# Linear attention and a GELU feed-forward block on one core: where the loads of batch 4 are issued

## The chip, the core and the metric

The kernel runs on one core of a Trainium2 chip. A core has five engines with queues of their own: PE (TensorE, matrix products into PSUM), DVE (VectorE), ACT (ScalarE), POOL (GpSimd) and SP (SyncE, which here issues nearly all DMAs). [...] The metric is the device time of one execution in microseconds, the median of several runs.

## The reference

For 8 batches, 8 heads, 576 positions and a head size of 64:

```python
q_s = softmax(q, axis=-1)          # over the 64 elements of a head
k_s = softmax(k, axis=2)           # over the 576 positions
kv  = einsum('bhsd,bhse->bhde', k_s, v)      # 64 x 64 per head
x   = einsum('bhsd,bhde->bhse', q_s, kv)     # then (4608 tokens, 512)
h   = x @ w_in                               # 512 -> 2048
g   = 0.5 * h * (1 + erf(h / sqrt(2)))       # exact GELU
out = g @ w_out                              # 2048 -> 512
```

All inputs and the output are float32. The kernel works in bfloat16 inside and accumulates in float32.

## The kernel before

**Chunks.** The 4608 tokens are cut into nine chunks of 512. Chunks 0 to 7 hold the first 512 positions of each batch, chunk 8 the last 64 positions of all eight. For each chunk there are two long phases on PE. `h_phase(c)` (matmuls at L295) computes the 16 column blocks of `x @ w_in`, four matmuls each, and ACT applies GELU to each block (L300) into `g`. `y_phase(c)` (matmuls at L305) computes four output groups `j` of 16 matmuls each, `g @ w_out`. The end of each group is `y_out(c, ps, j)`: DVE copies the group from PSUM to SBUF (`y_sb`, L312), and SP sends it to DRAM (L315). The PSUM pool `psum_y` of these groups has two buffers, so group `j` needs the buffer of group `j - 2`. The SBUF pool of `y_sb` has four.

**The attention of the next batches** is put between these matmuls. For a batch `b`:

- `load(b)` issues three DMAs on SP: q (L90), k and v (both L98). Each of the three names has two SBUF buffers, so batch `b` takes the buffers of batch `b - 2`.
- `exp_q(b)` and `exp_k(b)` (L133, L138) run on ACT, between the GELUs of two chunks, since ACT must load another function table for them.
- `cast_v_all(b)` (L145) converts v to bfloat16 in four DVE instructions.
- `norm_q(b)` sums (L196) and inverts (L197) on DVE and multiplies on POOL or DVE (L198).
- `xbar_step(b)` (L231) transposes the normalised q by a DMA that SP issues; its result is `qT`.
- `kv_step(b)` computes `kv` on PE (L166) and normalises it on DVE; `x_all(b)` multiplies `qT` with it on PE (L251), and DVE and ACT copy the result out as `xT`, which the next `h_phase` reads.

**The order is written by hand.** The program runs under a manual schedule: each engine executes its own instructions in the order in which the Python code emits them, and SP's DMAs too. `ins` names, for a block of the `h_phase`, or for a pair (group, matmul) of the `y_phase`, the functions that are emitted right behind it. From chunk 2 on the loop at L555 sets these places: loads two batches ahead at the start of `h_phase(c)`, `cast_v_all` behind matmul 8 of the first output group, `norm_q` behind the first matmul of the second group, `xbar_step` behind the first of the fourth, and `x_all` and `kv_step` within the third. Chunk 1's output phase (L538) has a plan of its own, because it finishes batch 2 and starts batch 3 there. Chunk 2 begins with `front3` (L549), which normalises and transposes batch 3 and issues `load(4)`.

SP's order around the change is, before: output (1,0), transpose of batch 2, outputs (1,1), (1,2) and (1,3), transpose of batch 3, `load(4)`, output (2,0). Here (1,2) stands for output group 2 of chunk 1.

Of the kernel before, what the change touches and what calls it, by code (L numbers as in the profile page):

```python
# [16 lines left out]
def kernel(  # L17
# [65 lines left out]
    def load_main(b, name, t, parts=1):  # L83
        f = f32in.tile([128, 2048], FP32, tag=name + "f")
        f = f.rearrange("p (h f) -> p h f", h=H)
        st[b][name + "f"] = f
        src = t[b, :, 0:M, :].rearrange("h (p j) d -> p h (j d)", j=J)
        n = H // parts
        for i in range(parts):
            nc.sync.dma_start(out=f[:, i * n:(i + 1) * n, :], in_=src[:, i * n:(i + 1) * n, :])  # L90

    def load_pair(b, name, t, parts=1):
        f = f32in.tile([128, HP, NS * D], FP32, tag=name + "f")
        st[b][name + "f"] = f
        src = t[b].rearrange("h (p n) d -> (h p) (n d)", n=NS).rearrange("(x q) f -> q x f", q=128)
        n = HP // parts
        for i in range(parts):
            nc.sync.dma_start(out=f[:, i * n:(i + 1) * n, :], in_=src[:, i * n:(i + 1) * n, :])  # L98

    def load(b):  # L100
        load_main(b, "q", q)
        load_pair(b, "k", k)
        load_pair(b, "v", v)
# [40 lines left out]
    def cast_v(b, hp, eng=nc.vector):  # L144
        eng.tensor_copy(  # L145
            out=v_aug[b % 2][:, hp, :, 0:D],
            in_=st[b]["vf"][:, hp, :].rearrange("p (n d) -> p n d", n=NS),
        )

    def cast_v_all(b):  # L150
        for hp in range(HP):
            cast_v(b, hp)
# [30 lines left out]
    def kv_step(b):  # L183
        kv_mm(b, 0)
        kv_mm(b, 1)
        kv_norm(b, 0, 2)

    def norm_q(b, i=0, n=1, eng=None):

        eng = eng or nc.gpsimd  # L190
        eq = st[b]["eq"]
        w = H // n
        hs = slice(i * w, (i + 1) * w)
        qsum = small.tile([128, J, w], FP32, tag="qsum")
        recq = small.tile([128, J, w], FP32, tag="recq")
        nc.vector.reduce_sum(out=qsum, in_=eq[:, :, hs, :], axis=AX.X)  # L196
        nc.vector.reciprocal(recq, qsum)  # L197
        eng.tensor_tensor(  # L198
            out=eq[:, :, hs, :], in0=eq[:, :, hs, :],
            in1=recq.unsqueeze(3).to_broadcast([128, J, w, D]), op=ALU.mult,  # L200
        )
# [27 lines left out]
    def xbar_step(b):  # L229
        st[b]["qT"] = attn_sb.tile([128, J, HP, 128], BF16, tag="qT", name="qT")  # L230
        nc.sync.dma_start_transpose(  # L231
            out=st[b]["qT"].rearrange("p j x m -> p (j x) m"),
            in_=st[b]["eq"].rearrange("p j h d -> p (j h d)"),
        )
# [27 lines left out]
    def x_all(b):  # L262

        for hp in range(HP):
            pool, tag = (psum_h, "h") if hp < 3 else (psum_a, "a")
            x_tile(b, hp, pool, tag)
        x_mm(b, 0)
        x_mm(b, 1)
        for hp, eng in ((0, "s"), (2, "v"), (1, "s"), (3, "v")):
            x_evac(b, hp, eng)  # L270
# [233 lines left out]
    def y_end(j):  # L504
# [35 lines left out]
        (1, 1): [lambda: norm_q(2, 1, 2, nc.vector)],  # L540
        (1, 12): [lambda: kv_step(2)],
        (1, 15): [lambda: xbar_step(2)],
        (2, 2): [lambda: cast_v_all(3)],
        (3, 5): [lambda: x_all(2), lambda: kv_step(3)],
    })

# [2 lines left out]
    def front3():  # L549
        norm_q(3, 0, 2)  # L550
        norm_q(3, 1, 2, nc.vector)
        xbar_step(3)
        load(4)

    for c in range(2, B + 1):  # L555
        nb = c + 2
# [54 lines left out]
```

The softmax here doesn't subtract the row's maximum and nothing guards it: scores larger than these inputs give would overflow.

## Time and profile before

| | |
|---|---|
| median of 3 runs | 283.63 us (283.61 to 283.81) |
| profiled execution, its own time | 283.85 us |
| its span, from the first to the last instruction | 282.0 us |
| PE busy | 272.0 us (96%) |
| ACT busy | 156.8 us (56%) |
| DVE busy | 102.1 us (36%) |
| granted PE clock | 1.0 throughout |
| one load of a batch: q, k, v | 1024, 1152 and 1152 KB |
| median time from issue to landing: q, k, v | 7.2, 9.8 and 11.5 us |
| one output group | 256 KB, 2.3 us to landing |
| one transposing DMA | 3.8 us to landing |

All times inside the profile are microseconds from the start of the span. A row of instruction groups reads: line, engine, operation, output <- inputs, shape, count; then the busy time and the mean of one in ns; then the idle time of the engine just before, and who ended it. A row of the waits reads: who waited for whom, in total, how often, the longest. A row of a timeline reads: start, duration, engine, line, operation, count, and in brackets the idle time of the engine before it. PE's matmuls are pipelined and their ends are modelled, so a stretch that is listed as busy can end some tenths of a microsecond late.

### The profile page before, as it was taken

To read this page: it belongs to the slowest core of one execution; us is meant where nothing else is said; L and a number is where in the kernel's file an instruction comes from. 1 tells how busy PE (TensorE), PEld (TensorE's weight loads), DVE (VectorE), ACT (ScalarE), POOL (GpSimd) and SP (SyncE) were. 2 spreads that over 40 slices of the span, in tenths; PEclk is the share of its full clock that TensorE was granted. 3 is DMA by queue.
4 is the path that set the end of the run, shared out by engine and by line. 5 is a ranking of instruction groups with operands and counts; after the bars stand their busy time and mean duration, and the time that the engine had idled before them with its cause. 6 is when DMAs were issued, how large, how long until landed. Compare 5 with 4: busy or idle time off the path is not lost.

```text
span 282.0 us, 4555 instructions
## 1 busy us (share of the span) xinstructions
PE 272.0 (96%) x1922; PEld 125.8 (45%) x1922; DVE 102.1 (36%) x150; ACT 156.8 (56%) x242; POOL 32.9 (12%) x25
## 2 busy tenths in 40 slices
PE   7789999999999899999999999999999999999993
PEld 3334454444444344444444444444444444444442
DVE  3766486309750560084007500651016100220021
ACT  5856754689377815693469446853683363136300
POOL 0620050002020050005000500050005000000000
PEclk9999999999999999999999999999999999999999
DMA  7999999952439339911991189117501500210033
GB/s 233 387 404 431 397 401 406 402 219 68 124 103 360 132 114 248 349 38 42 241 377 52 40 200 361 76 73 185 115 0 74 149 2 0 77 74 0 0 77 76
DMA packets 44852, 50.10 MB, mean 178 GB/s; under 512 B 20384, under 2 KB 29856, under 8 KB 44576
## 3 DMA queue, kind: packets, MB, share of 16 engines
q1 hardware_dynamic: 44544, 49.68, 51.8%
q8 instruction: 15, 0.25, 0.3%
q10 hardware_dynamic: 288, 0.13, 0.2%
q14 instruction: 5, 0.04, 0.0%
HBM read 36.70 MB, written 9.44 MB: 164 GB/s over the span
## 4 chain that ended last, share of the span: by engine, by line
PE 81%; DMA 10%; DVE 3%; ACT 2%; SPq 1%; issue 1%; ACTq 0%
PE ps L305 39%; PE ps L295 38%; DMA f<-in_v_dram 6%; DMA w<-in_moe_w_in_dram 3%; PE kv L166 2%; DMA f<-in_q_dram 1%; PE ps L251 1%; PE ps L327 1%; DVE v_aug L145 1%; DVE qsum L196 1%; ACT ek L138 1%; ACT e L133 1%; DVE e L198 1%; SPq L231 0%; DVE y_sb L312 0%
## 5 line engine op out<-in xcount | busy, mean ns | idle before, releaser
L295 PE MATMUL ps<-xT,wi_bf 128*128 128x512 bf16 x576 | 126.1, 379 | 1.0 <-DVE wi_bf L379 1.0
L305 PE MATMUL ps<-wo_bf,g 128*128 128x512 bf16 x560 | 124.4, 379 | 1.1 <-DVE y_sb L312 1.1
L300 ACT ACTIVATE g<-ps 128x512 bf16<-128x512 f32 x144 | 85.6, 597 | 68.4 <-PE ps L295 68.4
L295 PEld LDWEIGHTS <-wi_bf 128*128 128x128 bf16 x576 | 56.2, 98 | 69.3 <-DVE wi_bf L379 1.5
L305 PEld LDWEIGHTS <-g 128*128 128x128 bf16 x560 | 53.9, 98 | 65.5 <-issue 1.8
L312 DVE COPY y_sb<-ps 128x512 f32<-128x512 f32 x35 | 23.9, 684 | 74.9 <-PE ps L305 74.6
L198 POOL TENSOR_TENSOR e<-e,recq 128x2048 bf16<-128x2048 bf16 (+1 forms) x9 | 25.7, 2856 | 179.1 <-DVE recq L197 147.1
L145 DVE CAST v_aug<-f 128x576 bf16<-128x576 f32 x26 | 17.9, 745 | 57.1 <-DMA f<-in_v_dram 57.1
L277 ACT CAST xT<-ps 128x512 bf16<-128x512 f32 x19 | 10.2, 589 | 31.3 <-PE ps L251 21.7
L196 DVE TENSOR_REDUCE qsum<-e 128x16 f32<-128x1024 bf16 (+1 forms) x13 | 21.0, 1614 | 14.8 <-ACT e L133 14.8
L133 ACT ACTIVATE e<-f 128x512 bf16<-128x512 f32 (+1 forms) x42 | 20.5, 556 | 2.0 <-DMA f<-in_q_dram 1.7
L138 ACT ACTIVATE ek<-f 128x2304 bf16<-128x2304 f32 (+1 forms) x10 | 17.2, 1730 | 1.7 <-DMA f<-in_k_dram 1.7
L275 DVE CAST xT<-ps 128x512 bf16<-128x512 f32 x15 | 9.7, 687 | 15.4 <-PE ps L251 12.6
L79 ACT ACT_TABLE_LOAD x9 | 11.5, 1283 | 2.8 <-issue 2.6
L405 PE MATMUL ps<-zeros 128*128 128x512 f32 (+1 forms) x14 | 8.3, 734 | 1.5 <-DVE zeros L436 1.5
L133 ACT ACT_TABLE_LOAD x7 | 9.0, 1283 | 0.1
L379 DVE CAST wi_bf<-w 128x512 bf16<-128x512 f32 (+1 forms) x8 | 7.1, 909 | 2.8 <-DMA w<-in_moe_w_in_dram 2.8
L166 PEld LDWEIGHTS <-ek 64*64 64x64 bf16 x576 | 6.5, 105 | 2.9 <-issue 1.1
L166 PE MATMUL kv<-v_aug,ek 64*64 64x65 bf16 x576 | 7.1, 193 | 0.1
L398 DVE CAST wo_bf<-w 128x2048 bf16<-128x2048 f32 (+1 forms) x5 | 5.1, 1011 | 4.1 <-DMA w<-in_moe_w_out_dram 4.1
L198 DVE TENSOR_TENSOR e<-e,recq 128x1024 bf16<-128x1024 bf16 x4 | 6.4, 1610 | 0.1
L251 PE MATMUL ps<-qT,kvc 64*64 64x512 bf16 x60 | 5.0, 390 | 1.0 <-DVE kvc L177 1.0
(33 smaller groups left out, 41.6 us busy)
## 6 DMA issues: line engine op xcount, KB each, us to landing
out_dram<-y_sb SPq DMA_DIRECT2D x32, 256.0 KB, 2.3
f<-in_k_dram SPq DMA_DIRECT2D x6, 1152.0 KB, 9.8
f<-in_v_dram SPq DMA_DIRECT2D x6, 1152.0 KB, 11.5
f<-in_q_dram SPq DMA_DIRECT2D x6, 1024.0 KB, 7.2
w<-in_moe_w_in_dram SPq DMA_DIRECT2D x6, 512.0 KB, 8.9
f<-in_k_dram SPq DMA_DIRECT2D x4, 576.0 KB, 10.0
f<-in_v_dram SPq DMA_DIRECT2D x8, 288.0 KB, 7.7
f<-in_q_dram SPq DMA_DIRECT2D x4, 512.0 KB, 8.6
```

Source lines behind the costliest of these rows:

```text
L79: nc.scalar.activation(out=scr[:, 1:2], in_=scr[:, 0:1], func=func)
L133: nc.scalar.activation(out=dst[:, i], in_=src[:, u], func=AF.Exp)
L138: nc.scalar.activation(out=ek[b % 2][:, i:i + n], in_=st[b]["kf"][:, i:i + n].rearrange("p x (n d) -> p x n d", n=NS), func=AF.Exp,)
L145: eng.tensor_copy(out=v_aug[b % 2][:, hp, :, 0:D], in_=st[b]["vf"][:, hp, :].rearrange("p (n d) -> p n d", n=NS),)
L166: nc.tensor.matmul(ps[c, i, half, 0:D + 1], ek[b % 2][pr, hp, n, :], v_aug[b % 2][pr, hp, n, 0:D + 1], start=(n == 0), stop=(n == NS - 1),)
L196: nc.vector.reduce_sum(out=qsum, in_=eq[:, :, hs, :], axis=AX.X)
L198: eng.tensor_tensor(out=eq[:, :, hs, :], in0=eq[:, :, hs, :], in1=recq.unsqueeze(3).to_broadcast([128, J, w, D]), op=ALU.mult,)
L277: nc.scalar.copy(out=st[b]["xT"][:, hp, :], in_=ps)
L295: nc.tensor.matmul(ps, wi_bf[:, dm, t * 128:(t + 1) * 128], xT[:, dm, :], start=(dm == 0), stop=(dm == NDM - 1),)
L300: nc.scalar.activation(out=g[:, t, :], in_=ps, func=AF.Gelu)
L305: nc.tensor.matmul(ps, st[c]["g"][:, t, j * 128:(j + 1) * 128], wo_bf[:, t, :], start=(t == 0), stop=(t == NDF - 1),)
L312: nc.vector.tensor_copy(out=y_sb, in_=ps)
```

## The change

`load(4)` is issued in the third output group of chunk 1, behind its third matmul and the four casts of batch 3's v. Before, it was issued in the first block of chunk 2's `h_phase`, behind the transpose of batch 3. The three DMAs are the same, and no instruction is added or removed. In SP's order they now stand behind output (1,1) and ahead of outputs (1,2) and (1,3) and of the transpose of batch 3.

```diff
@@ y_phase(1, ...)
         (1, 12): [lambda: kv_step(2)],
         (1, 15): [lambda: xbar_step(2)],
-        (2, 2): [lambda: cast_v_all(3)],
+        (2, 2): [lambda: cast_v_all(3), lambda: load(4)],
         (3, 5): [lambda: x_all(2), lambda: kv_step(3)],
     })
@@ front3, called behind the first block of h_phase(2)
         norm_q(3, 0, 2)
         norm_q(3, 1, 2, nc.vector)
         xbar_step(3)
-        load(4)
```

## The prediction

> **What bounds the kernel now.** I read the page first, then the waits of TensorE, then the chain that ended last in order of time, then the timelines of PE and SP around the change. The page's first part, and its row for the second product (the `y` matmuls):
>
> ```profile
> PE 272.0 (96%) x1922; PEld 125.8 (45%) x1922; DVE 102.1 (36%) x150; ACT 156.8 (56%) x242; POOL 32.9 (12%) x25
> ...
> L305 PE MATMUL ps<-wo_bf,g 128*128 128x512 bf16 x560 | 124.4, 379 | 1.1 <-DVE y_sb L312 1.1
> ```
>
> PE is busy for 96% of the span at full clock. No other engine passes 56%. So the time moves only if an idle stretch of PE goes away or a new one appears. All of PE's listed waits:
>
> ```profile
> PE ps L405 <- DVE zeros L436: 1.5, 1, 1.5
> PE ps L305 <- DVE y_sb L312: 1.1, 1, 1.1
> PE ps L295 <- DVE wi_bf L379: 1.0, 1, 1.0
> PE ps L251 <- DVE kvc L177: 1.0, 2, 0.6
> PE ps L212 <- POOL e L198: 0.9, 1, 0.9
> ```
>
> The second is a single stall. The chain in order of time shows what is behind it (start us, us, what):
>
> ```profile
> 81.74 1.33 SPq L231
> ...
> 83.12 0.64 SPq L90
> ...
> 83.81 0.70 SPq L98
> ...
> 84.55 10.19 DMA f<-in_v_dram
> ...
> 94.76 2.73 DVE v_aug L145 x4
> 97.49 0.61 DVE y_sb L312
> ...
> 98.14 2.97 PE ps L305 x13
> ```
>
> These are the three DMAs of `load(4)` (L90 is q, L98 is k and then v), issued behind the transposing DMA of batch 3 (L231). `v` lands at 94.74. DVE casts it at once (`cast_v_all(4)`, four casts, 2.73 us), and only then copies out the first `y` group of chunk 2 (L312). PE's third group needs that group's PSUM buffer, since `psum_y` has two, and waits for it. The PE timeline of chunks 2, 3 and 4 gives the size of the loss:
>
> ```profile
> 89.95 7.07 PE L305 MATMUL ps<-wo_bf,g 128*128 128x512 bf16 x32
> 98.14 2.97 PE L305 MATMUL ps<-wo_bf,g 128*128 128x512 bf16 x13 [1.13 <-DVE y_sb L312]
> ...
> 106.35 13.98 PE L295 MATMUL ps<-xT,wi_bf 128*128 128x512 bf16 x64
> 120.16 9.88 PE L305 MATMUL ps<-wo_bf,g 128*128 128x512 bf16 x45
> ...
> 135.28 13.98 PE L295 MATMUL ps<-xT,wi_bf 128*128 128x512 bf16 x64
> 149.09 9.88 PE L305 MATMUL ps<-wo_bf,g 128*128 128x512 bf16 x45
> ```
>
> The output phase of chunk 2 runs from 89.95 to 106.35, 16.40 us. That of chunk 3, with the same instructions on PE, runs from 120.16 to 135.28, 15.12 us. The difference is 1.28 us: the 1.13 us listed, and 0.15 us by which the modelled end of the last matmul hides the stall's beginning. In chunk 3 DVE's cast starts only 0.49 us after the phase does (120.65), in chunk 2 it starts 4.81 us after.
>
> **What the Trainium skill says.** "PSUM — Partial Sum Buffer", section Engine vs sequencer instructions: VectorE's queue is strict FIFO. The trace agrees: the copy whose input was complete at about 93.6 (chunk 3 puts it 3.65 us after the phase's start) ran at 97.41, behind the casts. "DMA: Bandwidth & Descriptors", section Queues, rings and completion order: on each DMA engine a queue's descriptors are consumed in ring order, though a later one may finish its write first. So a load issued behind a transposing DMA on SP's queue should add no wait of its own in front of it. The trace shows the landings that I use below (3.7 to 3.9 us for all seven transposes, whatever follows them). The same page, section Rules for kernel authors, says that a transposing DMA next to ordinary DMAs needs nothing, so I expect no added wait between them; before has none in SP's list of waits.
>
> **The change part by part.**
>
> *Removed from chunk 2.* Three DMA issues on SP at 83.12 to 85.06 and their 3.3 MB. Nothing else stands behind them on SP there until the outputs of chunk 2 at 98.12, so SP gains nothing that matters.
>
> *Added to the output phase of chunk 1.* SP's order becomes transpose(2), output (1,1), `load(4)`, outputs (1,2) and (1,3), transpose(3). The SP timeline of before, and the first use of what the transpose gives on PE:
>
> ```profile
> 68.27 1.97 SPq L231 DMA_TRANSPOSE qT<-e  x1
> 70.33 7.05 SPq L315 DMA_DIRECT2D out_dram<-y_sb  x3
> ...
> 72.77 0.63 PE L251 MATMUL ps<-qT,kvc 64*64 64x512 bf16 x8
> ```
>
> Output (1,1) is issued by 70.33 + 0.33 = 70.66. The buffers that `load(4)` writes are those of batch 2. Their last readers are done: `exp_q(2)` by 64.50, `exp_k(2)` by 66.45 (half of the 4.12 us from 64.39), `cast_v_all(2)` by 53.77. So q is issued at 70.70, k at 71.39, v at 72.13, and SP is free at 72.64 (0.64 + 0.70 + 0.51 us and two gaps of 0.05). In before v landed 10.2 to 11.9 us after its issue, the longer ones behind an output. So v lands at 82.3 to 84.0, not at 94.74.
>
> *Cast of v(4).* On DVE it stands behind `norm_q(3)`, which ends at 81.60, so it runs from about 84 to 86.7, with DVE idle there (it now sits idle for 13.2 us until v lands). The stall vanishes if v lands before 97.02 (where PE ran dry) − 0.68 (copy) − 2.73 (casts) = 93.6. The margin is 9.6 us. **Gain: 1.28 us.**
>
> *What is late next in that phase.* The second group's copy waits for `norm_q(4)`'s sum on DVE, which waits for `exp_q(4)` on ACT until 94.25; ACT's place is fixed by the Gelus, not by the loads. Sum 2.28 and reciprocal 0.35 end at 96.9, and the copy at 97.6. PE needs that buffer for its fourth group at 89.95 + 3 × 3.46 = 100.3. Margin 2.7 us, exactly chunk 3's pattern, which shows no stall. So nothing takes the place: 0.
>
> *The DMAs that `load(4)` is moved ahead of.* Output (1,2), ready on DVE at 72.49, is issued at about 72.7 and lands behind the load, by about 84 and not by 75.3. Its SBUF buffer is reused four outputs later, at about 99: 0. Transpose(3) is still issued at 81.74, when `norm_q(3)` is done. At worst it lands behind the load's tail, 84.0 + 3.9 = 87.9. It is needed at 101.04 − 1.28 = 99.8: 0.
>
> *The transpose that `load(4)` is moved close behind.* Transpose(2) is issued at 68.27 and takes 3.9 us, so it lands at 72.17, and PE starts `x_all(2)` with it at 72.77: cover 0.60 us. This is the only thin one. Lower bound of the cost: 0, as for transpose(3) in before, where q followed 1.38 us behind the issue (here 2.43 us) and the landing was 3.9 us too. Upper bound, if from q's issue on the load takes half of the DMA: the remaining 72.17 − 70.70 = 1.47 us becomes 2.94, landing at 73.64, stall 0.87. I take 0.
>
> *Sum* on the profiled execution: span 282.0 − 1.28 = 280.8, and with the 1.8 us around it (283.85 − 282.0) 282.57. That execution lies 0.22 us above the median of the three runs. Against the median: 283.63 − 1.28 = **282.35 us** (−0.45%). A measurement of this kernel tells about 0.2% (0.57 us) from no change.
>
> **The rivals.**
>
> 1. *The transpose shares the DMA with the load* (stall 0.87, above): 283.63 − 1.28 + 0.87 = 283.2, within 0.2%. For it: the cover is only 0.60 us, and the DMA engines are full while a transpose runs. Against it: the ring order, and the seven landings within 0.2 us of each other.
>
> 2. *The transpose is held back by the load: slower.* The place is the same, PE at 72.77. It decides when transpose(2) lands more than 0.60 + 1.28 = 1.88 us late, i.e. takes over 5.8 us. If only a third of the DMA were left to it from 70.70 on, the landing would be at 75.11, the stall 2.34, and the time 283.63 − 1.28 + 2.34 = 284.7. Against it: no transpose in before took over 3.9 us.
>
> 3. *Another wait takes the place of the one removed, or the load is held on SP:* 283.6. For it: in before the k of `load(3)`, among much other traffic, took SP 4.8 us to issue, so a full queue can hold SP; and two engines meet in that phase. Against it: even 4.8 us for each of three issues puts v's issue at about 80 and its landing at 90 to 92, before 93.6; and the `norm_q(4)` path has 2.7 us. This is also the rival that the change doesn't do what it says; the buffers being free speaks against it.
>
> **How the numbers follow.** Likeliest case 0.85; rival 1 0.05; rival 2 0.06; rival 3 0.04. Range 282.0 to 283.0: below, the forecast less the spread of a run (0.2) and a little more for a stall whose start the model hides; above, a gain of about half, which covers a transpose that lands late by up to 1.25 us (0.60 covered and 0.65 paid). The cases past it hold under 0.2. Chances: faster 0.86, within 0.2% 0.08 (rival 3 and most of rival 1), slower 0.06 (rival 2).
>
> **What would show it.** In the profile after: PE's wait for `y_sb` gone, and the output phase of chunk 2 at 15.1 us; v's DMA issued near 72.1 and landed before 85; DVE's casts of batch 4 right behind `norm_q(3)`; PE without a wait at `x_all(2)`; chunks 3 to 8 as before but 1.28 us earlier. The prediction is wrong if PE shows idle time in front of L251 near 72.8, waiting for a DMA, if the transpose takes well over 4 us, or if a wait for `y_sb` stays.

## The result, and the profile after

The changed kernel takes 281.65 us (median; 280.69 to 282.4) against 283.72 us of the kernel before. The ratio is 0.992, with a 95% interval of 0.9897 to 0.9942. That is 2.07 us faster. The forecast was 1.28 us faster, 282.35 us, with a range of 282.0 to 283.0. So the direction was right and the time lies below the range.

The page of the changed kernel, with the two rows that were shown of before:

```profile
PE 271.2 (97%) x1922; PEld 125.6 (45%) x1922; DVE 102.5 (37%) x150; ACT 156.8 (56%) x242; POOL 32.9 (12%) x25
...
L305 PE MATMUL ps<-wo_bf,g 128*128 128x512 bf16 x560 | 124.2, 379 | 0.0
```

The row of the second product has no idle time any more. All waits of PE:

```profile
PE ps L212 <- POOL e L198: 1.5, 1, 1.5
PE ps L405 <- DVE zeros L436: 1.5, 1, 1.5
PE ps L295 <- DVE wi_bf L379: 1.0, 1, 1.0
PE ps L251 <- DVE kvc L177: 1.0, 2, 0.6
```

The wait for `y_sb` is gone; what is left lies in the first 20 us of the kernel, as before. The chain that ended last no longer passes through `load(4)`. Where it had the loads, the casts and the copy, it now stays on PE (start us, us, what):

```profile
74.13 2.27 PE ps L305 x10
76.40 13.81 PE ps L295 x64
90.21 9.71 PE ps L305 x45
```

PE's timeline around the moved load shows that nothing took its place:

```profile
72.87 0.63 PE L251 MATMUL ps<-qT,kvc 64*64 64x512 bf16 x8
...
76.23 13.98 PE L295 MATMUL ps<-xT,wi_bf 128*128 128x512 bf16 x64
90.05 9.88 PE L305 MATMUL ps<-wo_bf,g 128*128 128x512 bf16 x45
```

`x_all(2)` at 72.87 starts without a wait. The output phase of chunk 2 begins at 90.05 and runs its 45 matmuls up to `x_all(3)` in 9.88 us, as chunk 3 did before. SP's timeline shows the new order (the load between the two transposes), and DVE's what became of the cast:

```profile
68.37 1.82 SPq L231 DMA_TRANSPOSE qT<-e  x1
...
70.87 0.44 SPq L90 DMA_DIRECT2D f<-in_q_dram  x1
71.40 0.65 SPq L98 DMA_DIRECT2D f<-in_k_dram  x1
72.10 0.51 SPq L98 DMA_DIRECT2D f<-in_v_dram  x1
...
81.84 4.57 SPq L231 DMA_TRANSPOSE qT<-e  x1
```

```profile
85.20 2.73 DVE L145 CAST v_aug<-f 128x576 bf16<-128x576 f32 x4 [3.50 <-DMA f<-in_v_dram]
93.70 0.69 DVE L312 COPY y_sb<-ps 128x512 f32<-128x512 f32 x1 [5.77 <-PE ps L305]
```

The three DMAs of `load(4)` are issued at 70.87, 71.40 and 72.10. `v` lands 13.1 us after its issue, at 85.2, and DVE casts it then. The copy that PE waited for in before runs at 93.70, when its input is complete, and nothing stands ahead of it.

**Where the other part comes from.** PE's last stretch of matmuls starts at 272.80 in the changed kernel and at 273.99 in before: 1.19 us earlier. This is the forecast gain of 1.28 less 0.10, by which this execution got through its start more slowly (chunk 1's first product starts at 46.11, not 46.01). But the span shrank by 2.16 us, from 282.04 to 279.88. The remaining 0.97 us lie behind PE's last matmul. From the start of DVE's last copy to the end of the span it is 4.36 us in before (277.68 to 282.04) and 3.39 us in the changed kernel (276.49 to 279.88). The DMAs of this last stretch, first of before, then of the changed kernel (queue, packets, MB, share; then the issues with size and time to landing):

```profile
q14 instruction: 1, 0.01, 0.4%
...
out_dram<-y_sb SPq DMA_DIRECT2D x1, 96.0 KB, 2.1
out_dram<-y_sb ACTq DMA_DIRECT2D x1, 96.0 KB, 2.8
out_dram<-y_sb SPq DMA_DIRECT2D x1, 32.0 KB, 2.9
out_dram<-y_sb ACTq DMA_DIRECT2D x1, 32.0 KB, 3.1
```

```profile
q14 instruction: 1, 0.01, 0.5%
...
out_dram<-y_sb SPq DMA_DIRECT2D x1, 96.0 KB, 2.1
out_dram<-y_sb ACTq DMA_DIRECT2D x1, 96.0 KB, 2.4
out_dram<-y_sb SPq DMA_DIRECT2D x1, 32.0 KB, 1.9
out_dram<-y_sb ACTq DMA_DIRECT2D x1, 32.0 KB, 2.1
```

The work of this stretch is the same in both, yet in before the last 32 KB on SP's queue take 2.9 us to land and not 1.9, and those on ACT's queue 3.1 and not 2.1. In both there is one transfer of an instruction queue (q14), 8 KB. In the trace's list of DMA packets, before has this fetch at 279.56 to 279.89, in the middle of the last outputs. Of SP's last 32 KB, all packets but five have started by 279.60; these five start between 279.89 and 279.98, right behind the fetch. Five more, of ACT's last 32 KB, start between 279.99 and 280.26. Each of the two 32 KB outputs is 64 packets of 512 bytes and 16 of 4 bytes in the trace; the five that lag are four and one of these, a sixteenth. That points to one of the core's 16 DMA engines, though the trace doesn't name the engine of a packet. In the changed kernel the fetch comes at 276.85, ahead of these outputs, and no packet lags. From the last data packet to the landing of the last output it is 0.81 us in before and 0.36 us in the changed kernel; from that landing to the end of the span it is 0.96 us in both. That the fetch holds up the last output was the theory to be tested.

### The profile page after: what moved, and what is told of

Its sections match the earlier page's. It is cut to its first block, busy times and chain, and to the rows that moved or that the text cites. A ratio compares the mean times of both kernels' runs of the same rounds, so it can differ in the third digit from the quotient of the medians.

```text
span 279.9 us, 4557 instructions
## 1 busy us (share of the span) xinstructions
PE 271.2 (97%) x1922; PEld 125.6 (45%) x1922; DVE 102.5 (37%) x150; ACT 156.8 (56%) x242; POOL 32.9 (12%) x25
## 4 chain that ended last, share of the span: by engine, by line
PE 75%; DMA 20%; ACT 2%; SPq 1%; DVE 0%; ACTq 0%; issue 0%
PE ps L305 36%; PE ps L295 35%; DMA w<-in_moe_w_in_dram 6%; DMA f<-in_k_dram 5%; DMA f<-in_v_dram 4%; DMA out_dram<-y_sb 3%; DMA touch<-in_moe_w_out_dram 2%; PE kv L166 1%; PE ps L327 1%; PE ps L251 1%; ACT ek L138 1%; ACT e L133 1%; ACTq L423 0%; ACT L133 0%; SPq L98 0%; DVE v_aug L145 0%
## 5 line engine op out<-in xcount | busy, mean ns | idle before, releaser
L405 PE MATMUL ps<-zeros 128*128 128x512 f32 (+1 forms) x14 | 7.6, 686 | 1.5 <-DVE zeros L436 1.5
## 6 DMA issues: line engine op xcount, KB each, us to landing
f<-in_v_dram SPq DMA_DIRECT2D x8, 288.0 KB, 7.5
```

## The experiments

Every ratio is to the kernel before, timed beside the run. Two theories on the unforecast part were put to the chip: theory T, the collision of an instruction fetch with the last output, whose place depends on the program; and rival R, scatter from execution to execution.

**e1 and e2: both kernels again.** No edit.

> The kernel before, unchanged, profiled a second time. Two theories on the part of the gain that was not forecast (2.07 us measured, 1.28 forecast; the profiles put 0.97 us of it behind PE's last matmul). Theory T (a fixed collision at the end): an 8 KB instruction fetch falls among the packets of the last output DMA. It then shows again here: from the start of DVE's last copy to the end of the span 4.3 us (4.36 in the first profile of before), the fetch after that copy by 1.9 us, ratio 1.000. Rival R (scatter of the executions): the end differs from the first profile by some tenths, anywhere between 3.4 and 4.4 us.

> The changed kernel, unchanged, profiled a second time. Theory T: from the start of DVE's last copy to the end of the span 3.4 us again, the 8 KB fetch 0.4 us after that copy's start, ratio 0.992 to 0.993. Rival R: the end anywhere between 3.4 and 4.4 us, and a ratio near 0.9955 (1.28 us of 283.6) when enough executions are compared.

Measured: 283.48 against 283.74 us, ratio 0.9995 (0.9985 to 1.0005), and 281.32 us, ratio 0.9917 (0.9894 to 0.9939). The ends were 4.38 and 3.41 us, with the fetch 1.90 and 0.36 us behind the start of DVE's last copy. So the end belongs to the program, and rival R is out. One thing differed: in e1 the stall of PE was 1.51 us, not 1.13, and the output phase of chunk 2 lasted from 89.95 to 106.73, 16.78 us. Against 15.12 that is a loss of 1.66 us, where the first profile gave 1.28.

**e3 and e4: one instruction more on DVE or SP**, with a new small tile.

```diff
+    pad = singles.tile([16, 8], FP32)
...
+        if c == 5:
+            ins[4] = [lambda: nc.vector.memset(pad, 0.0)]     # e3
+            ins[4] = [lambda: nc.sync.dma_start(out=pad[:, 0:2], in_=moe_w_in[0:128:8, 0:2])]     # e4
```

> The kernel before with one inert DVE instruction more, a memset of a small tile that nobody reads, emitted in chunk 5 where DVE is idle. It moves DVE's instruction stream by one. Theory T with the fetch being DVE's: the fetch moves against the last output and the end shrinks by 0.8 to 1.0 us, ratio about 0.997, with PE's timeline unchanged. Theory T with the fetch being another engine's, and rival R: ratio 1.000, the fetch stays 1.9 us behind DVE's last copy.

> The kernel before with one inert DMA of 128 bytes more on SP, emitted in chunk 5, into a tile that nobody reads. It moves SP's instruction stream by one DMA and perhaps a wait. Theory T with the fetch being SP's: the end shrinks by 0.8 to 1.0 us, ratio about 0.997, with PE's timeline unchanged. Theory T with the fetch being another engine's, and rival R: ratio 1.000.

Measured: 285.61 us, ratio 1.008 (1.0051 to 1.0109), and 287.0 us, ratio 1.0118 (1.0092 to 1.0145). Both are slower, which no theory had said. The ends fit T with the fetch being DVE's: 3.64 us in e3, 4.33 in e4. But the rest of the kernel had changed too, in both: the stall of PE in chunk 2 grew, and PE was slow behind it. In e4:

```profile
100.56 4.65 PE L305 MATMUL ps<-wo_bf,g 128*128 128x512 bf16 x13 [2.19 <-DVE y_sb L312]
```

13 matmuls take 4.65 us; in before the same 13 took 2.97. The stretches of this time (their lengths, each engine's busy time, then the granted PE clock, the DMA share and GB/s) show why:

```profile
100.50:102.50 2.00, 1.94 (x7) 0.79 (x7) 2.00 (x2) 0.00 (x0) 0.00 (x0) 0.70 0.33 123
102.50:105.00 2.50, 2.50 (x8) 0.78 (x6) 1.10 (x3) 0.00 (x0) 1.71 (x1) 0.56 0.21 73
```

The granted clock was 0.70 and 0.56 in these stretches, after a stall of 2.19 us. What the two kernels have in common is the new tile, 32 bytes per partition, which by the program moves the tiles allocated behind it (the traces don't show addresses). e5 and e6 repeat the test without it, e7 and e8 test the shift alone.

**e5: one DVE instruction more, no new tile.**

```diff
     nc.vector.memset(scr, 0.0)
-    for i in range(2):
+    for i in (0, 1, 1):
         nc.vector.memset(v_aug[i][:, :, :, D:D + 1], 1.0)
```

> The kernel before, with one of DVE's first memsets (v_aug's column of ones) issued twice, at the start, where DVE has nothing to do. No tile is added, so no address in SBUF moves, unlike in e3. DVE's stream grows by one instruction. Theory T (the 8 KB fetch at the end is DVE's, and its place in DVE's stream decides whether it collides with the last output): the fetch comes 0.3 to 0.5 us after the start of DVE's last copy and not 1.9, the end shrinks from 4.4 to 3.4 us, the stall of PE at 97 us stays (1.1 to 1.5 us), ratio 0.9965 (-0.97 us). Rival (the end was shortened by the moved load itself): ratio 1.000, end 4.4 us.

Measured: 282.52 us, ratio 0.9959 (0.9944 to 0.9974), end 3.42 us. The stall of PE is still there, and the last outputs land early (the wait of PE, then the DMAs of the end):

```profile
PE ps L305 <- DVE y_sb L312: 1.1, 1, 1.1
```

```profile
out_dram<-y_sb ACTq DMA_DIRECT2D x1, 96.0 KB, 2.4
out_dram<-y_sb SPq DMA_DIRECT2D x1, 32.0 KB, 2.0
out_dram<-y_sb ACTq DMA_DIRECT2D x1, 32.0 KB, 2.1
```

A second memset of the same ones at the start of the kernel, where DVE has nothing to do, makes it about 1.1 us faster. It adds one instruction to DVE's stream and nothing else; chunk 1's first product starts at 45.99, as in before (46.01).

**e6: the changed kernel with one DVE instruction fewer.**

```diff
     for i in range(2):
-        nc.vector.memset(v_aug[i][:, :, :, D:D + 1], 1.0)
+        (nc.gpsimd if i else nc.vector).memset(v_aug[i][:, :, :, D:D + 1], 1.0)
```

> The changed kernel, with one of DVE's first memsets given to POOL: DVE's stream is one instruction shorter, as long as in the kernel before. Theory T: the collision at the end comes back, end 4.4 us, fetch 1.9 us behind the start of DVE's last copy; ratio to before 0.9955 (the forecast gain of 1.28 us alone) and not 0.992. Rival: ratio 0.992, end 3.4 us.

Measured: 282.12 us, ratio 0.9952 (0.9933 to 0.9972), end 4.36 us. The collision is back, with before's landings:

```profile
out_dram<-y_sb ACTq DMA_DIRECT2D x1, 96.0 KB, 2.8
out_dram<-y_sb SPq DMA_DIRECT2D x1, 32.0 KB, 2.9
out_dram<-y_sb ACTq DMA_DIRECT2D x1, 32.0 KB, 3.1
```

The forecast gain alone would be a ratio of 0.9955. So e5 holds the part that was not forecast, and e6 the part that was: 0.41% and 0.48%, together 0.89%, where the whole change measured 0.80 to 0.83%; the intervals, 0.15 and 0.2 to either side, cover the difference.

The list of all kernels leaves no exception. "DVE" is the number of DVE's instructions in the trace, with its semaphore waits, which the page's x150 leaves out; fetch, last packet and end are counted from the start of DVE's last copy, in us:

| kernel | DVE | fetch | last packet | end |
|---|---|---|---|---|
| before, e1 | 194 | 1.87, 1.90 | 2.60, 2.62 | 4.36, 4.38 |
| e4, e7 | 194 | 1.92, 1.90 | 2.62, 2.62 | 4.33, 4.39 |
| e6 | 194 | 1.88 | 2.60 | 4.36 |
| after, e2 | 195 | 0.35, 0.36 | 2.07, 2.03 | 3.39, 3.41 |
| e3, e5, e8 | 195 | 0.37, 0.37, 0.37 | 2.14, 2.05, 2.04 | 3.64, 3.42, 3.43 |
| e9, e10, e11, e12 | 195 | 0.42, 0.34, 0.35, 0.36 | 2.04, 2.13, 2.03, 2.04 | 3.43, 3.54, 3.41, 3.41 |

So the change does add instructions, contrary to what was said of it: the Python code has none more, but the built program has one semaphore wait more on DVE and one on SP (the pages count 4557 instructions, and 4555 before). SP's doesn't matter: e4 and e6 have as many on SP as the changed kernel and the long end, and e3, e5, e11 and e12 have no more than before and the short one. DVE's is a wait at 85.21 of line 312, for the copy that stands behind the casts of batch 4's v. In before the first of these casts itself waits for that semaphore. e10, e11 and e12 have the same added wait.

What the runs show is that the number of DVE's instructions sets the place of the fetch and the length of the end. That it is DVE's fetch is concluded from this, and that the fetch holds back the packets behind it is read from their order in the trace. The Trainium skill, "Runtime: NRT & Kernel Launch", section Instruction fetch mechanics, says that each engine's sequencer fetches the next block of its stream by DMA while it executes the present one. The trace agrees that such fetches go by DMA. The page gives blocks of 16 KiB; here every fetch on q14 is a packet of 8 KB. Why one instruction moves this fetch by 1.5 us, from 0.4 to 1.9 us behind the copy, is open.

**e7 and e8: the shift of the addresses alone**, on the kernel before and on the changed one. The same edit in both:

```diff
-    touch = singles.tile([16, 4, 2], FP32)
+    touch = singles.tile([16, 4, 4], FP32)
...
-        nc.scalar.dma_start(out=touch[:, i, :], in_=a)
+        nc.scalar.dma_start(out=touch[:, i, 0:2], in_=a)
```

> The kernel before, with one tile of 16 partitions 32 bytes per partition larger, so that all tiles allocated behind it stand 32 bytes further in SBUF; the instructions are the same. e3 and e4 had such a shift too, and in both the loads were slower, the stall of PE grew to 2.1 to 2.2 us, and PE ran 13 matmuls behind it in 4.65 us, not 2.97. Theory S (the shift of the addresses makes the loads slower): as in e4, stall about 2.2 us, 13 matmuls in 4.65 us, ratio 1.010 to 1.013. Rival (the added DMA or DVE instruction did it): ratio 1.000.

> The changed kernel with the same shift of 32 bytes. If the moved load takes v of batch 4 off PE's path, slower loads can't stall PE in chunk 2: no wait for y_sb, output phase of chunk 2 15.1 us. What is left of the shift's cost is the later start of chunk 1 (about 1.0 us in e3 and e4): about 282.4 us, ratio 0.995 to 0.996, so about 4 us below e7. If the slower loads reach PE in another place, it shows as a new wait and e8 loses as much as e7.

Measured: e7 286.4 us, ratio 1.0114 (1.0084 to 1.0143); e8 283.06 us, ratio 0.9976 (0.9966 to 0.9987). The instructions of e7 are those of before. The DMA rates of the pages, in 40 slices, first of e1, then of e7:

```profile
GB/s 247 399 390 430 398 400 406 403 202 81 110 108 351 134 105 238 366 39 39 235 368 66 42 201 361 70 77 179 120 0 74 149 2 0 77 74 0 0 77 75
```

```profile
GB/s 236 378 383 418 373 392 378 373 321 44 148 64 316 210 76 205 367 58 76 199 374 55 74 179 332 119 76 157 141 0 74 147 2 0 76 74 0 0 76 75
```

In slices 2 to 8, where the inputs and weights are loaded, the means are 404 and 385 GB/s: 5% less. All four kernels with the shift (e3, e4, e7, e8) have 384 to 385 there, all ten profiles without it 403 to 405. The stall of PE in e7 is the 2.1 us that was expected:

```profile
PE ps L305 <- DVE y_sb L312: 2.1, 1, 2.1
```

In the profiled execution of e7 the 13 matmuls behind it ran at full clock, in 2.96 us; so a stall of that length doesn't cost the clock each time. It did in the profiled executions of e3 and e4, which have a mean clock of 0.994 and 0.993. Of e3's other executions four had 1.0 and took 285.0 to 285.7 us, and one 0.994 and 287.4; of e7's, two had 0.992 and 0.994 and took 287.9 and 288.0, against 285.6 to 286.5 in the rest. In e8 there is no wait for `y_sb`, and PE runs the output phase of chunk 2 up to `x_all(3)` in 9.88 us without a stop. The change takes 3.3 us off a kernel whose loads are slower by 5%, and 2.1 to 2.4 us off one whose loads are not. e8 is 0.7 us above what was expected. For 0.4 of this the traces have the place: the shift costs 1.4 us in chunks 0 and 1 (the output phase of its chunk 2 begins at 91.47, that of the changed kernel at 90.05), not 1.0.

**e9: the load one step earlier still**, ahead of the transpose of batch 2.

```diff
-        (1, 12): [lambda: kv_step(2)],
+        (1, 12): [lambda: kv_step(2), lambda: load(4)],
...
-        (2, 2): [lambda: cast_v_all(3), lambda: load(4)],
+        (2, 2): [lambda: cast_v_all(3)],
```

> load(4) one step earlier still: behind kv_step(2) in the second output group of chunk 1, so that SP issues it ahead of the transpose of batch 2 and not behind it. It measures what the thin cover of 0.60 us would cost on the wrong side. Theory Q (the transpose waits in SP's DMA queue behind the 3.3 MB): q is issued at about 65.9, v at 67.3, the loads hold the queue to about 75.7, the transpose lands at 77 to 80 and not at 72.1, and PE stalls 5 to 8 us ahead of x_all(2); the 1.28 us in chunk 2 are still gained. 287 to 291 us, ratio 1.012 to 1.026. Rival (the transpose shares the DMA engines with the load evenly): it lands at about 76, stall 3 to 4 us, ratio about 1.007.

Measured: 291.99 us, ratio 1.0288 (1.0258 to 1.0318). Worse than expected, in the direction of theory Q. SP's timeline and PE's:

```profile
65.92 0.39 SPq L90 DMA_DIRECT2D f<-in_q_dram  x1
66.55 0.51 SPq L98 DMA_DIRECT2D f<-in_k_dram  x1
67.11 0.50 SPq L98 DMA_DIRECT2D f<-in_v_dram  x1
68.28 11.40 SPq L231 DMA_TRANSPOSE qT<-e  x1
```

```profile
81.77 1.07 PE L251 MATMUL ps<-qT,kvc 64*64 64x512 bf16 x8 [8.91 <-DMA qT<-e]
82.58 1.25 PE L166 MATMUL kv<-v_aug,ek 64*64 64x65 bf16 x72
84.16 3.58 PE L305 MATMUL ps<-wo_bf,g 128*128 128x512 bf16 x9 [0.33 <-issue]
```

The transpose is issued at 68.28, 2.36 us after q, and lands 13.5 us later, at 81.7, not 3.7 to 3.9. PE waits 8.91 us for it. Behind the wait the granted clock was 0.50 from 81 to 85 us: `x_all(2)`, `kv_step(3)` and the rest of the phase take from 81.77 to 87.58, 5.81 us, where before took from 72.77 to 76.13, 3.36. The sum: `x_all(2)` starts 9.00 us later, the slower clock costs 2.45, the stall in chunk 2 is gone (1.28), and the end is 0.93 shorter (3.43 and not 4.36). That makes 9.2 us, the difference of the spans (291.3 and 282.0). The expectation missed the clock, and put the landing of the transpose 2 to 5 us too early. `v` of batch 4, the last DMA ahead of the transpose in SP's order, landed at 79.8, and the transpose 2.0 us later; SP took 11.40 us to issue it.

**e10: the two lines of `front3` exchanged**, on the kernel before.

```diff
+        load(4)
         xbar_step(3)
-        load(4)
```

> The kernel before, with the two lines of front3 exchanged: load(4) ahead of the transpose of batch 3. SP then need not wait for norm_q(3) with it: q is issued at about 77.5, v at 78.9, v lands at 88 to 90. The prediction's threshold says that the stall is gone when v lands before 93.6: no wait for y_sb, output phase of chunk 2 15.1 us. The transpose of batch 3 lands at 88 to 91, needed at 99.8. Ratio 0.9955 with an end of 4.4 us, 0.992 with one of 3.4 us. If the early place in chunk 1 matters by itself, the gain is smaller.

Measured: 281.42 us, ratio 0.9908 (0.9883 to 0.9933), with an end of 3.54 us. DVE's timeline:

```profile
90.34 2.73 DVE L145 CAST v_aug<-f 128x576 bf16<-128x576 f32 x4 [8.59 <-DMA f<-in_v_dram]
93.77 0.69 DVE L312 COPY y_sb<-ps 128x512 f32<-128x512 f32 x1 [0.69 <-PE ps L305]
```

`v` lands at 90.3, the casts end at 93.07, and the copy runs at 93.77, on time. The threshold of the prediction (v landed by 93.6 for no stall) is met with 3 us to spare, DVE is free 0.7 us before the copy is due. The transpose of batch 3, now behind the load, landed at 92.2, 10.3 us after its issue and 1.9 us after `v`, a little later than expected and still in time. Chunk 1 as the place of the load is not needed for the gain.

**e11: the load left where it was, the cast moved behind the copy**, on the kernel before.

```diff
             yi[(1, 0)] = [lambda nb=nb: norm_q(nb)]
-            if nb < B:
+            if nb == 4:
+                yi[(1, 0)].append(lambda: cast_v_all(4))
+            elif nb < B:
                 yi[(0, 8)] = [lambda nb=nb: cast_v_all(nb)]
```

> The kernel before, the load left where it was; cast_v_all(4) emitted behind norm_q(4) of the second output group and not behind matmul 8 of the first, so that DVE's copy of the first group stands ahead of it. Theory D (PE stalled because DVE's queue put the cast, waiting for v, ahead of that copy): the copy runs at 93.6, no wait for y_sb, the cast runs from 97 to 99.7 and is done before kv_step(4); PE as in the changed kernel. Ratio 0.9955 with an end of 4.4 us, 0.992 with one of 3.4 us. Rival (PE is held by something that only an earlier load removes): ratio 1.000.

Measured: 281.23 us, ratio 0.9919 (0.9893 to 0.9946), end 3.41 us. DVE's timeline:

```profile
93.24 0.69 DVE L312 COPY y_sb<-ps 128x512 f32<-128x512 f32 x1 [12.01 <-PE ps L305]
93.92 2.29 DVE L196 TENSOR_REDUCE qsum<-e 128x32 f32<-128x2048 bf16 x1
96.31 0.35 DVE L197 RECIPROCAL recq<-qsum 128x32 f32<-128x32 f32 x1
96.58 2.67 DVE L145 CAST v_aug<-f 128x576 bf16<-128x576 f32 x4
99.16 0.68 DVE L312 COPY y_sb<-ps 128x512 f32<-128x512 f32 x1
```

The copy runs at 93.24, the cast behind `norm_q(4)` from 96.58 on, and PE has no wait there. So PE had stalled because of DVE's order: a cast that waited for a DMA stood ahead of a copy whose input was ready. An earlier load is one cure, another place for the cast is as good a one.

**e12: v alone loaded early.**

```diff
-        (2, 2): [lambda: cast_v_all(3), lambda: load(4)],
+        (2, 2): [lambda: cast_v_all(3), lambda: load_pair(4, "v", v)],
...
         xbar_step(3)
+        load_main(4, "q", q)
+        load_pair(4, "k", k)
```

> One part of the change alone: only v of batch 4 is loaded in chunk 1; its q and k stay behind the transpose of batch 3. If v alone counts: as the changed kernel, no wait for y_sb, v landed by 78; q and k land at 89 and 92, before exp_q(4) at 92.1 and exp_k(4) at 94.2. Ratio 0.992, if the end is 3.4 us, else 0.9955. If q or k counts too, ACT's exp waits and the ratio is nearer to 1.

Measured: 281.51 us, ratio 0.9914 (0.9895 to 0.9933), end 3.41 us, no wait for `y_sb`. `v` landed at 76.8, q and k at 88.8 and 91.6, in time for their exps. The early load of v is enough for the gain. Of e10, e11, e12 and the changed kernel none can be told from the others by time. All four have DVE's extra instruction, so all four have both parts of it.

## Why the prediction was right or wrong

- **The stall and its cause: right.** The wait for `y_sb` is gone, and the output phase of chunk 2 is as long as chunk 3's. e11 shows the mechanism (DVE's order), e10 the threshold, e12 that v is what counts.
- **Its size: right within the scatter.** 1.28 us came from one profiled execution. A second profile of before gave 1.66, e5 gave 1.20 (89.93 to 106.25), since v lands at other times in other executions (the casts start at 94.76, 95.15 and 94.67). e6, which has this part alone, measured 0.48% (0.28 to 0.67%), 1.36 us.
- **When v lands: forecast 1.2 us too early, without effect.** Forecast 82.3 to 84.0, measured 85.2; it had until 93.6.
- **What could take the stall's place: right, nothing did.** Sum and copy of the second group ran as in chunk 3.
- **The transposes: right where it mattered.** That of batch 2 landed after 3.7 us, so rivals 1 and 2 didn't come about. That of batch 3 took 6.6 us and landed at 88.4, half a microsecond later than the bound of 87.9, and long before it was needed at 99.8. The bound added a transpose's own 3.9 us to the landing of the load. But outputs (1,2) and (1,3) also stand ahead of this transpose in SP's order and landed behind the load, (1,3) at 86.5, and the transpose landed 1.9 us after that. In e9 and e10, too, it landed 2.0 and 1.9 us after the last DMA ahead of it. So in these three kernels the place in SP's order sets when a transpose lands, and even sharing does not fit: for e9 it would have given 76, and the landing was at 81.7. e9 also shows what a transpose that is held back costs here: not the 1.06 us given for rival 2 but 8.2 us.
- **The sum: wrong.** The step that failed is the one that carried the gain to the end unchanged ("chunks 3 to 8 as before but 1.28 us earlier", and the span less 1.28). PE did come to its end 1.19 us earlier, but the stretch behind PE's end was taken as fixed, and it shrank by 0.97 us. The change adds a semaphore wait to DVE's stream, with it the fetch of DVE's last 8 KB of instructions comes ahead of the last output DMA and not in its midst, and the last 32 KB land a microsecond sooner. e5 and e6 show from both sides that it is the count of DVE's instructions, and the table shows it in all kernels. With this term, known only afterwards, the sum is 283.63 − 1.28 − 0.97 = 281.38; the change measured 281.65, and e2 281.32. This part of the gain is luck: it comes from one instruction more, not from the load's place.
- **The range: its lower end had only the scatter of the executions in it**, and no term for the end of the kernel. The profile of before had a sign there: the last 32 KB took 2.9 and 3.1 us to land, more than the 2.1 and 2.8 of three times as much issued just ahead of them.

Of the 0.97 us, 0.53 are the later end of the last packet (2.60 against 2.07 us behind the copy's start). The rest, 0.44, lies between the last packet and its landing (0.81 against 0.36); why that takes longer in before is open.

## What to carry to other kernels

When PE waits for a copy out of PSUM, look at what stands ahead of that copy in DVE's queue. If it is an instruction that waits for a DMA, load earlier or put that instruction behind the copy; both gave the same here. A load that is moved in SP's order must be placed by what it is put ahead of: just behind the transpose of batch 2 it cost nothing, just ahead of it the kernel was 8 us slower than before. Ahead of the transpose of batch 3 (e10) it cost nothing either: that one still landed more than 7 us before it was needed. And when a forecast is a few tenths of a percent, look at the stretch behind the last matmul as well, since one instruction more or fewer on DVE moved it by 1 us, whatever the instruction was for.

## What the runs showed of the hardware that was not expected

- The trace lists an engine's instruction fetches among the packets of the core's DMA engines. With one of 8 KB in the midst of the last output's packets the end of the kernel was 0.97 us longer, and one inert DVE instruction moved it ahead of them (e5: ratio 0.9959).
- A shift of the tiles behind `touch` by 32 bytes per partition took 5% off the rate of the loads (404 to 385 GB/s) and cost 1.1% of the time (e7), with no instruction more or fewer.
- A transposing DMA behind other DMAs of SP landed 1.9 to 2.0 us after the last of them (changed kernel, e9, e10), up to 13.5 us after its own issue; the seven of before took 3.7 to 3.9.
- A stall of PE of 2.1 to 2.2 us can cost more than its length. In the profiled executions of e3 and e4 the granted clock fell behind it (0.70 and 0.56 in e4), and 13 matmuls took 4.65 us, not 2.97; in that of e7 it did not. The Trainium skill, "TensorE: Matmul & The Clock Gate", section What's actually happening, gives an idle window of about 3.4 us, free-running, for the clock to fall; here it fell after less, and the measurement decides.
